# A planner's costs raised a little for each ScalarE, VectorE and GpSimd instruction and each DMA

## The chip, the cores and the metric

The kernel runs on one core of one Trainium2 chip. The metric is the device time of one execution in microseconds (us), the median of several runs. Engines are named as in the profile: PE (TensorE matmuls), PEld (its weight loads), ACT (ScalarE), DVE (VectorE), POOL (GpSimd), SP (SyncE, which issues the DMAs).

## The reference

```python
q_n, k_n = rmsnorm(q, g_q), rmsnorm(k, g_k)            # q, k, v: 4 batches, 12 heads, 448 x 64
attn = softmax(q_n @ k_n.T / sqrt(64))                 # the row maximum is subtracted first
x = (attn @ v).transpose(0, 2, 1, 3).reshape(1792, 768)
h = maximum(x @ w_in, 0); x = (h * h) @ w_out          # first MLP, 768 -> 2048 -> 768
h = x @ w_in2                                          # second MLP, same sizes
out = (maximum(h, 0) + alpha * minimum(h, 0)) @ w_out2
```

## The kernel before

All data is 32-bit. A product of two fp32 matrices is made of three fp32r matmuls: each operand is split into a high part (a copy that rounds) and a low part (the rest), and high x high, high x low and low x high are added in PSUM. So nearly every matrix needs a copy (L254 on ACT, L258 on DVE, L256 on POOL) and a subtraction (L262 on DVE or POOL) before PE may read it. A matmul has 128x128 weights and 448 columns, one batch's tokens.

The program has two parts. `with_attention` does attention for the four batches, head by head: norms (L528 to L611), spreading of the norm factors (L636, L641), splitting of q and k into tiles `mv` and `st` (L254, L262), a matmul for the row maximum (L685) that DVE reduces (L689), transposes (L692), scores (L710), exponentials (L718), the product with v (L729 in fp32, L753 in three parts) and the division (L766 to L783). Between these stand the matmuls of the first MLP for batches 0 and 1 (L350, `bank<-xs,whl` and `bank<-hg,whl`). They are PE's other work while a head waits for ACT and DVE. Their weights come in units. The first time, a unit is loaded (`raw`), converted by ACT (L282) and four DVE instructions (L286, L289, L293, L296) into `ws`, split by L254 and L262 into `whl`, and written back to DRAM. Later uses load the split form. The first pass has 56 units, on average 10.3 matmuls each (32 of 9 and 24 of 12).

`without` does the first MLP for batches 2 and 3 (L350, `m<-...`), and then the second MLP in two stages, first for batches 0 and 1, then for 2 and 3. A stage forms 2x2 blocks and takes seven products instead of eight: steps "up" (u0 to u7) and "down" (d0 to d2, each of three quads) of seven products of six or nine matmuls (L984), into PSUM banks `n`. Between the products ACT copies banks out (L254, `q<-n`, `ws<-n`), DVE adds (L995) and applies alpha (L1022), and the sums are split into `forms`. Weight sums are L908. `x_pair` prepares a stage's input: it loads four blocks of the first MLP's result `y` (`q<-y`, `ws<-y`), and with DVE or POOL subtractions (L995) and splits (L254, L262) makes seven forms in `xs` and `xt`. It does so three times for a stage. Copies of banks and loads of `y` take their space from one pool, `q`, of nine slots; those whose space lies in the old `ws` tile are printed as `ws`. The second stage's inputs are prepared while PE does the last step of the first, d2: I call this place the join.

No order is written by hand. `Tasks.add` records every instruction with an urgency, the engines that can do it and the time it is expected to take (`act`, `dve`, `dve2`, `pool1`, `pool2`, `load`, `MM` = 0.202). `Tasks.run` (L104 to L187) plays them through on a model with one clock for each engine: among the tasks that can begin soonest it takes the most urgent, gives it an engine and buffer slots, and sets when the engine is free (`ends`) and when the result may be used (`t.end` plus WAIT). Instructions are emitted in that order. On the chip each engine then works its list from the top; the times of the model have no other part in it.

```python
WAIT = {"T": 0.27, "A": 0.17, "V": 0.17, "P": 0.17, "S": 0.1}
s = max(s, d.end + (0 if d.engine == e == "T" else self.WAIT[e]))
t.end = self.ends[e] = s + t.on[e]
```

Of the kernel before, what the change touches and what calls it, by code (L numbers as in the profile page):

```python
# [52 lines left out]
class Tasks:  # L53
    WAIT = {"T": 0.27, "A": 0.17, "V": 0.17, "P": 0.17, "S": 0.1}

    PRICE = {"A": 1.5, "V": 3.5, "P": 1.5}
# [44 lines left out]
    def run(self, phase=0):  # L101
# [16 lines left out]
        while left:  # L118
# [42 lines left out]
            if e == "S" and t.on[e]:  # L161
                self.ends[e] = s + 0.06
                self.dma = max(self.dma, s + 1.3) + t.on[e]
                t.end = self.dma + 0.8
            else:
                t.end = self.ends[e] = s + t.on[e]
                self.gap[e] = t.gap
                if e in t.alone:
                    self.port = t.end
# [49 lines left out]
def attention_relu2_mlp_prelu_mlp(ctx: ExitStack, tc: tile.TileContext, qkt, qk_tm, v, gb, alpha, ident, sel,  # L219
# [199 lines left out]
    def with_attention():  # L419
        with ExitStack() as es:  # L420
# [70 lines left out]
            def attention(b, base, first=False):  # L491
# [17 lines left out]
                def first_norms(pairs, urgency, r):  # L509
# [3 lines left out]
                    for p in pairs:  # L513
                        src, sq = load_qk(p), Buf(pool=here("pf"))
                        for i in range(2):
# [3 lines left out]
                            def square(e, src=src, rows=rows, i=i):  # L519
# [6 lines left out]
                            n = steps.index((p, i))  # L526
                            add(urgency, {"T": 4 * MM},
                                lambda e, n=n, rows=rows: nc.tensor.matmul(  # L528
# [25 lines left out]
                def norms(gr):  # L554
# [57 lines left out]

                    add(urgency, {"T": 0.4}, transposes, [t1, ident_b], [pr])
                    for o in (0, 64):
# [64 lines left out]
                def shift(h):  # L679

                    m, s, mc, mn = mvs[h], sts[h], Buf(pool="mc"), Buf(pool="mn")
                    for t in range(NCH):
# [8 lines left out]
                    pt = Buf(pool="bank")  # L691
                    add(at(h, -19), {"T": 0.1}, lambda e: nc.tensor.transpose(pt.ap[:NCH, :CP], mc.ap, ident_b.ap),  # L692
                        [(mc, t) for t in range(NCH)], [pt])
# [5 lines left out]
                def head(h):  # L699
                    p, j = divmod(h, 2)  # L700
                    m, s, o = mvs[h], sts[h], Buf(pool="pv")
                    for n in range(NCH):
# [17 lines left out]
                        if p not in vparts:  # L720
                            if n % 2 == 0:
                                pf = Buf(pool=here("pf"))

                            def pfv(pf=pf, c=n % 2 * S, keys=keys):
                                return pf.ap[:keys, c:c + S]

                            add(g, {"A": act(S, True)}, exp(pfv), [pa], [(pf, n % 2)], "exp")
                            add(at(h, 5 + n), {"T": 4 * MM},
                                lambda e, n=n, pfv=pfv, keys=keys: nc.tensor.matmul(  # L729
                                    out=o.ap[:, :S], lhsT=vs[p].ap.bitcast(F32)[:keys, 192 * n + 64 * j:192 * n + 64 * j + 128], rhs=pfv(),  # L730
                                    start=(n == 0), stop=(n == NCH - 1)), [(pf, n % 2), vs[p]], [o], "pv")
                            continue
# [515 lines left out]
```

## Time and profile before

| | us |
|---|---|
| median of 3 runs (1257.81 to 1262.97) | 1258.88 |
| the profiled execution | 1263.64 |
| its span | 1261.9 |
| PE busy | 1193.9 (95%) |
| DVE busy | 890.5 (71%) |
| ACT busy | 771.2 (61%) |
| POOL busy | 506.9 (40%) |

Busy PE isn't PE at its peak, since matmuls are pipelined and a waiting one can look busy; the number of matmuls in a stretch is the better measure. PE has 5466 records, of which 1008 are of the group L984 `n<-forms,whl`. The chain that ended last is 60% PE, 20% DVE, 9% ACT, 7% DMA.

### The profile page before, as it was taken

Reading aid. Unit: us, or ns where it says so; the run is one execution under the profiler, and the core shown is the slowest. Engines: PE = TensorE matmul, PEld = TensorE weight load, DVE = VectorE, ACT = ScalarE, POOL = GpSimd, SP = SyncE. Lnnn points to the kernel's source line nnn. Section 1 sums busy time; section 2 is a strip of 40 time slices with the busy share of each in tenths; the row PEclk is TensorE's granted clock in tenths of the full one; section 3 lists DMA queues with packets and bytes.
Section 4 is the critical chain, followed back from the end, with each engine's and each line's share of the span. In section 5 each row is a group of like instructions: output and inputs, shape, how many; then the busy total and the mean of one; then the engine's idle time right before and its main releaser. Section 6 shows DMA issues by size and latency. Waiting matters only on the chain.

```text
span 1261.9 us, 17161 instructions
## 1 busy us (share of the span) xinstructions
PE 1193.9 (95%) x5466; PEld 1006.7 (80%) x5466; DVE 890.5 (71%) x1593; ACT 771.2 (61%) x1543; POOL 506.9 (40%) x469
## 2 busy tenths in 40 slices
PE   4898999999999999999999999999999979999998
PEld 2555676666679888898989999888989869898987
DVE  6888999989996864603787661088776996847483
ACT  5787789777778777822555311376746745654472
POOL 4345345564355323310000002864676743317255
PEclk7998999999999999999999999999999989999999
DMA  6325767677754445267999996482616548261632
GB/s 203 101 82 179 235 240 276 217 267 257 243 213 133 158 150 174 91 204 255 320 342 308 320 362 207 169 277 96 251 50 241 184 141 260 77 200 52 211 109 81
DMA packets 95803, 250.32 MB, mean 198 GB/s; under 512 B 11296, under 2 KB 30880, under 8 KB 95712
## 3 DMA queue, kind: packets, MB, share of 16 engines
q1 hardware_dynamic: 95712, 249.22, 58.1%
q8 instruction: 43, 0.70, 0.2%
q14 instruction: 48, 0.39, 0.1%
HBM read 178.32 MB, written 70.78 MB: 197 GB/s over the span
## 4 chain that ended last, share of the span: by engine, by line
PE 60%; DVE 20%; ACT 9%; DMA 7%; issue 3%; SPq 0%; POOL 0%; ACTq 0%; DVEq 0%
PE n L984 23%; PE m L350 14%; PE bank L350 10%; PE pv L729 4%; PE bank L710 4%; DMA raw<-in_w 3%; DVE mc L689 2%; PE pv L753 2%; DVE n L995 2%; PE bank L685 2%; DMA whl<-w 2%; DVE ws L293 2%; DVE ws L296 2%; DVE ws L286 1%; ACT forms L254 1%
## 5 line engine op out<-in xcount | busy, mean ns | idle before, releaser
L984 PE MATMUL n<-forms,whl 128*128 128x448 f32 x1008 | 212.4, 371 | 17.1 <-ACT ws L254 7.2
L984 PEld LDWEIGHTS n<-forms,whl 128*128 128x128 f32 x1008 | 190.7, 190 | 37.7 <-DVE forms L262 8.1
L350 PE MATMUL bank<-xs,whl 128*128 128x448 f32 x576 | 137.9, 379 | 0.4 <-DMA whl<-w 0.4
L350 PE MATMUL bank<-hg,whl 128*128 128x448 f32 x576 | 130.1, 367 | 0.8 <-DMA whl<-w 0.8
L984 PE MATMUL n<-xs,whl 128*128 128x448 f32 x576 | 123.1, 367 | 1.5 <-ACT ws L254 1.2
L262 POOL TENSOR_TENSOR whl<-ws,whl 128x384 fp32r<-128x384 f32 (+2 forms) x56 | 79.9, 1430 | 105.7 <-ACT whl L254 99.0
L350 PEld LDWEIGHTS bank<-xs,whl 128*128 128x128 f32 x576 | 108.5, 191 | 16.2 <-issue 4.2
L282 ACT ACTIVATE ws<-raw 128x384 f32<-128x384 f32 (+1 forms) x112 | 67.2, 600 | 85.7 <-DMA raw<-in_w 75.1
L350 PE MATMUL m<-xs,whl 128*128 128x448 f32 x576 | 118.3, 367 | 1.0 <-ACT q L254 0.7
L350 PE MATMUL m<-hg,whl 128*128 128x448 f32 x576 | 119.2, 368 | 0.0
L689 DVE TENSOR_REDUCE mc<-bank 112x1 f32<-112x448 f32 x192 | 109.8, 615 | 10.7 <-PE bank L685 9.5
L984 PEld LDWEIGHTS n<-xs,whl 128*128 128x128 f32 x576 | 107.8, 188 | 11.8 <-issue 1.5
L350 PEld LDWEIGHTS m<-xs,whl 128*128 128x128 f32 x576 | 107.9, 188 | 11.3 <-ACT q L254 1.1
L350 PEld LDWEIGHTS m<-hg,whl 128*128 128x128 f32 x576 | 108.1, 188 | 10.9
L350 PEld LDWEIGHTS bank<-hg,whl 128*128 128x128 f32 x576 | 107.3, 188 | 11.1 <-DMA whl<-w 1.5
L262 POOL TENSOR_TENSOR whl<-raw,whl 128x384 fp32r<-128x384 f32 (+1 forms) x87 | 90.0, 1038 | 51.1 <-ACT whl L254 43.1
L286 DVE TENSOR_SCALAR ws<-ws 128x384 f32<-128x384 f32 (+1 forms) x112 | 48.8, 442 | 86.2 <-ACT ws L282 85.8
L710 PE MATMUL bank<-mv,st 128*112 128x448 f32 (+2 forms) x352 | 102.1, 398 | 6.0 <-DVE mc L689 3.8
L262 POOL TENSOR_TENSOR xs<-q,xs 128x448 fp32r<-128x448 f32 x11 | 13.2, 1211 | 234.9 <-ACT xs L254 234.9
L254 ACT ACTIVATE whl<-raw 128x384 fp32r<-128x384 f32 (+1 forms) x123 | 60.7, 500 | 57.1 <-PE n L984 44.4
L984 PE MATMUL n<-xt,whl 128*128 128x448 f32 x432 | 94.0, 367 | 1.7 <-DVE q L995 1.2
L984 PEld LDWEIGHTS n<-xt,whl 128*128 128x128 f32 x432 | 80.8, 188 | 9.8 <-DVE q L995 1.6
(173 smaller groups left out, 2301.0 us busy)
## 6 DMA issues: line engine op xcount, KB each, us to landing
raw<-in_w SPq DMA_DIRECT2D x64, 384.0 KB
raw<-in_w SPq DMA_DIRECT2D x48, 512.0 KB
whl<-w SPq DMA_DIRECT2D x64, 384.0 KB
whl<-w SPq DMA_DIRECT2D x48, 512.0 KB
k_u<-whl SPq DMA_DIRECT2D x56, 384.0 KB
whl<-k_u SPq DMA_DIRECT2D x56, 384.0 KB
w<-whl SPq DMA_DIRECT2D x32, 384.0 KB
w<-whl SPq DMA_DIRECT2D x24, 512.0 KB
```

What stands on the lines that cost most here:

```text
L254: nc.scalar.activation(out=o, in_=i, func=ACTF.Copy)
L262: (nc.gpsimd if e == "P" else nc.vector).tensor_tensor(out=o, in0=x, in1=hi, op=ALU.subtract)
L282: lambda e: nc.scalar.activation(out=f.ap[:, :n], in_=half(1).bitcast(F32), func=ACTF.Abs), [raw], [f], "f")
L286: lambda e: nc.vector.tensor_scalar(out=f.ap[:, :n], in0=f.ap[:, :n], scalar1=TINY, scalar2=None, op0=ALU.max),
L293: lambda e: nc.vector.scalar_tensor_tensor(out=fu(), in0=half(1), scalar=0xC0000000, in1=fu(), op0=ALU.bitwise_and, op1=ALU.bitwise_or), [ ...
L296: lambda e: nc.vector.scalar_tensor_tensor(out=fu(), in0=half(0), scalar=29, in1=fu(), op0=ALU.logical_shift_right, op1=ALU.bitwise_or), [ ...
L350: nc.tensor.matmul(out=acc.ap[:, t, :S], lhsT=w.ap[:, part * n + 128 * kk:part * n + 128 * kk + 128], rhs=src(h, k0 + kk, t)[1](), start=( ...
L685: lambda e, t=t, pm=pm: nc.tensor.matmul(out=pm.ap[:CP, :S], lhsT=m.ap[:, 0, t * CP:(t + 1) * CP], rhs=s.ap[:, 0, :], start=True, stop=Tru ...
L689: lambda e, t=t, pm=pm: nc.vector.reduce_max(out=mc.ap[:, t:t + 1], in_=pm.ap[:CP, :S], axis=AX.X),
L710: nc.tensor.matmul(out=pa.ap[:keys, :S], lhsT=s.ap[:rows, k, c:c + keys], rhs=m.ap[:rows, k, :], start=(k == 0), stop=(k == 1))
L729: lambda e, n=n, pfv=pfv, keys=keys: nc.tensor.matmul(out=o.ap[:, :S], lhsT=vs[p].ap.bitcast(F32)[:keys, 192 * n + 64 * j:192 * n + 64 * j ...
L984: nc.tensor.matmul(out=psum(x), lhsT=w.ap[:, part * n + 128 * kk:part * n + 128 * kk + 128], rhs=get(h)[1](), start=fresh and h == 1, stop ...
```

## The change

A table LATE is added (in us), and its number goes onto the end of every task that takes time. On ACT, DVE and POOL the engine is also held longer (`ends`). For a DMA only the result comes later. Four PE tasks get other numbers: an fp32 matmul 0.751 instead of 0.808, two transposing tasks 0.32 instead of 0.4 and 0.035 instead of 0.1. No instruction's work changes; what changes is the order, which engine takes a task that several can do, and which slot a buffer gets. All line numbers from L56 on rise by 2.

```diff
     WAIT = {"T": 0.27, "A": 0.17, "V": 0.17, "P": 0.17, "S": 0.1}
+
+    LATE = {"T": 0.0, "A": 0.04, "V": 0.04, "P": 0.1, "S": 0.25}
...
-                t.end = self.dma + 0.8
+                t.end = self.dma + 0.8 + self.LATE[e]
             else:
-                t.end = self.ends[e] = s + t.on[e]
+                t.end = self.ends[e] = s + t.on[e] + self.LATE[e] * (t.on[e] > 0)
...
-                            add(urgency, {"T": 4 * MM},
+                            add(urgency, {"T": 0.751},
...
-                    add(urgency, {"T": 0.4}, transposes, [t1, ident_b], [pr])
+                    add(urgency, {"T": 0.32}, transposes, [t1, ident_b], [pr])
...
-                    add(at(h, -19), {"T": 0.1}, lambda e: nc.tensor.transpose(pt.ap[:NCH, :CP], mc.ap, ident_b.ap),
+                    add(at(h, -19), {"T": 0.035}, lambda e: nc.tensor.transpose(pt.ap[:NCH, :CP], mc.ap, ident_b.ap),
...
-                            add(at(h, 5 + n), {"T": 4 * MM},
+                            add(at(h, 5 + n), {"T": 0.751},
```

The first place is ACT at the join. `q_4644<-n_6534` copies the first product of d2's second quad out of its bank, and `ws<-n_6539` the second product; `xs` and `xt` rows are splits of prepared input. Before:

```order
L254 ACTIVATE q_4644<-n_6534 128x448
L254 ACTIVATE whl<-wf_6529 128x384 x2
L254 ACTIVATE xs_62<-q_6532 128x448
L254 ACTIVATE whl<-raw 128x384
L254 ACTIVATE xs_62<-ws 128x448
L254 ACTIVATE xs_63<-ws 128x448
L254 ACTIVATE xt_4639<-ws 128x448
L254 ACTIVATE ws<-n_6539 128x448
```

After, on ACT at the same place (the first product is copied to `q_6533`, the third by the last row):

```order
L256 ACTIVATE q_6533<-n_6540 128x448
L256 ACTIVATE xs_63<-q_4642 128x448
L256 ACTIVATE xt_4641<-q_4643 128x448
L256 ACTIVATE xt_4640<-q_4645 128x448
L256 ACTIVATE ws<-n_6539 128x448
L256 ACTIVATE whl<-wf_6529 128x384
L256 ACTIVATE xs_62<-q_4644 128x448
L256 ACTIVATE q_4642<-n_6540 128x448
```

Ahead of the second copy stand three splits of the first `x_pair` instead of seven instructions, four of which are splits of the second `x_pair`, whose `y` blocks are loaded late.

The second place is DVE at the join: from `sums_out<-n_...`, the last addition of d2's first quad, to the first addition of its second quad (`...<-n_6539`). Before there are 20 instructions between the two, among them four L908; these rows are the last eleven and the addition:

```order
L995 TENSOR_TENSOR ws<-ws,q_6532 128x448
L262 TENSOR_TENSOR xs_62<-q_6532,xs_62 128x448
L262 TENSOR_TENSOR xs_62<-ws,xs_62 128x448
L262 TENSOR_TENSOR xs_63<-ws,xs_63 128x448
L262 TENSOR_TENSOR xt_4639<-ws,xt_4639 128x448
L995 TENSOR_TENSOR ws<-ws 128x448
L995 TENSOR_TENSOR q_6532<-ws,q_6532 128x448
L995 TENSOR_TENSOR ws<-ws 128x448
L262 TENSOR_TENSOR xs_63<-ws,xs_63 128x448
L262 TENSOR_TENSOR xt_4641<-q_6532,xt_4641 128x448
L262 TENSOR_TENSOR xt_4640<-ws,xt_4640 128x448
L995 TENSOR_TENSOR ws<-n_6539,ws 128x448
```

After, on DVE, from the one addition to the other (12 instructions between):

```order
L997 TENSOR_TENSOR sums_out<-n_6534,sums_out 128x448
L264 TENSOR_TENSOR xt_4639<-ws,xt_4639 128x448
L997 TENSOR_TENSOR q_4642<-q_4642,ws 128x448
L260 CAST whl<-wf_6529 128x384
L997 TENSOR_TENSOR q_4643<-q_4642,q_4643 128x448
L997 TENSOR_TENSOR q_4645<-q_4645,q_4642 128x448
L264 TENSOR_TENSOR xs_63<-q_4642,xs_63 128x448
L264 TENSOR_TENSOR xt_4641<-q_4643,xt_4641 128x448
L264 TENSOR_TENSOR xt_4640<-q_4645,xt_4640 128x448
L910 TENSOR_TENSOR raw<-raw 128x384 x3
L997 TENSOR_TENSOR ws<-ws,q_4644 128x448
L997 TENSOR_TENSOR q_4642<-n_6539,q_4642 128x448
```

The work of the second `x_pair` has moved behind the addition, and a copy of weights (CAST) has come to DVE.

The third place is PE where batch 1's first heads begin; L685 (after: L687) is a head's matmul for the maximum, L350 (L352) the first MLP's. Before:

```order
L350 MATMUL bank_158<-xs_62,whl 128x448 x12
L685 MATMUL bank_159<-st_167,mv_163 112x448
L685 MATMUL bank_156<-st_167,mv_163 112x448
L350 MATMUL bank_158<-xs_62,whl 128x448 x3
L685 MATMUL bank_159<-st_167,mv_163 112x448
L350 MATMUL bank_157<-xs_62,whl 128x448 x3
L685 MATMUL bank_156<-st_167,mv_163 112x448
L350 MATMUL bank_157<-xs_62,whl 128x448 x3
```

After, on PE at the same place:

```order
L352 MATMUL bank_157<-xs_62,whl 128x448 x12
L687 MATMUL bank_156<-st_167,mv_163 112x448
L687 MATMUL bank_159<-st_167,mv_163 112x448
L687 MATMUL bank_156<-st_167,mv_163 112x448
L352 MATMUL bank_157<-xs_62,whl 128x448 x3
L687 MATMUL bank_159<-st_167,mv_163 112x448
L352 MATMUL bank_160<-xs_62,whl 128x448 x6
L687 MATMUL bank_156<-st_168,mv_164 112x448
```

Three of the first head's matmuls now stand together, and six MLP matmuls instead of three stand between the last of them and the second head's first. Counted in the order, the first MLP runs further ahead of attention later on: between the last L685 of the 24th head and that of the 32nd there are 252 MLP matmuls instead of 156.

## Rows read from the trace of the kernel before

**Rows 1.** Page, busy time of PE, share of the span, instructions

```profile
PE 1193.9 (95%) x5466; PEld 1006.7 (80%) x5466; DVE 890.5 (71%) x1593; ACT 771.2 (61%) x1543; POOL 506.9 (40%) x469
```

**Rows 2.** Stretches: length, busy PE, PEld, DVE, ACT, POOL, TensorE clock, DMA share, GB/s

```profile
115.00:355.00 240.00, 222.73 (x920) 163.48 (x921) 222.57 (x424) 190.81 (x396) 117.53 (x101) 0.98 0.70 242
355.00:580.00 225.00, 221.49 (x1077) 194.17 (x1075) 128.21 (x221) 150.56 (x313) 72.19 (x72) 1.00 0.50 162
580.00:818.00 238.00, 237.01 (x1153) 216.05 (x1152) 129.68 (x248) 91.69 (x136) 33.81 (x30) 1.00 0.85 291
...
990.00:1030.00 40.00, 29.93 (x130) 26.45 (x129) 35.58 (x53) 22.74 (x46) 21.98 (x19) 0.87 0.32 112
```

**Rows 3.** Timeline of PE at the join: start, length, work [idle before, releaser]

```profile
998.35 17.39 PE L984 MATMUL n<-forms,whl 128*128 128x448 f32 x75 [2.80 <-DVE forms L262]
1022.91 7.37 PE L984 MATMUL n<-forms,whl 128*128 128x448 f32 x27 [7.16 <-ACT ws L254]
```

**Rows 4.** Timeline of ACT at the join

```profile
1012.19 0.54 ACT L254 ACTIVATE q<-n 128x448 f32<-128x448 f32 x1 [1.50 <-PE n L984]
...
1016.54 1.14 ACT L254 ACTIVATE xs<-ws 128x448 fp32r<-128x448 f32 x2 [0.39 <-DMA ws<-y]
...
1022.31 0.54 ACT L254 ACTIVATE ws<-n 128x448 f32<-128x448 f32 x1 [2.16 <-DVE ws L995]
```

**Rows 5.** Timeline of DVE at the join

```profile
1010.30 0.62 DVE L995 TENSOR_TENSOR sums_out<-n,sums_out 128x448 f32<-128x448 f32 x1 [0.15 <-PE n L984]
...
1014.22 3.38 DVE L908 TENSOR_TENSOR raw<-raw 128x384 f32<-128x384 f32 x3
...
1021.61 0.61 DVE L995 TENSOR_TENSOR ws<-ws 128x448 f32<-128x448 f32 x1
```

**Rows 6.** Timeline of SP's queue behind the join

```profile
1028.79 0.34 SPq L265 DMA_DIRECT2D out_t<-sums_out  x1
1029.22 0.38 SPq L265 DMA_DIRECT2D q<-y  x1
```

**Rows 7.** Timeline of POOL at the join

```profile
1027.37 1.39 POOL L995 TENSOR_TENSOR sums_out<-sums_out,ws 128x448 f32<-128x448 f32 x1 [10.65 <-DVE ws L995]
```

**Rows 8.** Stretches of 10 us at the join, columns as in rows 2

```profile
1020.00:1030.00 10.00, 7.09 (x27) 6.43 (x28) 8.35 (x15) 4.62 (x10) 1.54 (x2) 0.68 0.04 13
1030.00:1040.00 10.00, 10.00 (x50) 9.09 (x49) 10.00 (x15) 6.08 (x13) 5.77 (x4) 1.00 0.64 202
```

**Rows 9.** Timeline of DVE: two copies of weights and a weight sum

```profile
834.62 0.35 DVE L258 CAST whl<-raw 128x384 fp32r<-128x384 f32 x1
...
992.89 1.17 DVE L258 CAST whl<-raw 128x384 fp32r<-128x384 f32 x1
...
996.45 0.55 DVE L908 TENSOR_TENSOR raw<-wf 128x384 f32<-128x384 f32 x1
```

**Rows 10.** Timeline of PE, first stage of the second MLP

```profile
832.09 2.09 PE L984 MATMUL n<-xt,whl 128*128 128x448 f32 x9 [1.19 <-DVE q L995]
...
918.15 4.09 PE L984 MATMUL n<-forms,whl 128*128 128x448 f32 x18 [1.15 <-DVE forms L262]
```

**Rows 11.** Timeline of DVE in the first 20 us

```profile
17.67 1.27 DVE L587 TENSOR_REDUCE ss<-tm 112x8 f32<-112x512 f32 x2
18.86 0.67 DVE L550 SCALAR_TENSOR_TENSOR rhl<-rhl,columns,r 128x448 fp32r<-128x448 f32 x1
```

**Rows 12.** PE's longest wait from 115 to 355: total us, times, longest

```profile
PE bank L685 <- ACT mv L254: 4.5, 1, 4.5
```

**Rows 13.** Groups of DVE's weight conversion: busy us, mean ns | idle before

```profile
L296 DVE SCALAR_TENSOR_TENSOR ws<-raw,ws 128x384 uint32<-128x384 uint32 (+1 forms) x112 | 71.3, 643 | 2.0
L293 DVE SCALAR_TENSOR_TENSOR ws<-raw,ws 128x384 uint32<-128x384 uint32 (+1 forms) x112 | 69.6, 628 | 1.9
L286 DVE TENSOR_SCALAR ws<-ws 128x384 f32<-128x384 f32 (+1 forms) x112 | 48.8, 442 | 86.2 <-ACT ws L282 85.8
L289 DVE TENSOR_SCALAR ws<-ws 128x384 uint32<-128x384 uint32 (+1 forms) x112 | 47.7, 432 | 2.1
```

## The prediction

> **What bounds the kernel now.** I read the page's busy times first: PE is busy for 1193.9 of 1261.9 us [rows 1], so 68.0 us are visible waits, and no other engine is near it. The matmuls stay the same, so only PE's waits and the clock that it is granted can change. Then I read the stretches, to see where the waits lie. From 580 to 818, where PE runs from one list of matmuls, 1153 of them take 238 us, 0.206 us each; the sparsest stretch is 990 to 1030, with 130 in 40 us, PE busy for 29.93 us, and a mean clock of 0.87 [rows 2]. From 115 to 355 PE is idle for 240 - 222.73 = 17.3 us, and DVE is busy for 222.57 of 240 us [rows 2]: there attention and the first MLP's weight conversion fill DVE. From 355 to 580 DVE is busy for 128.21 of 225 us, and PE is idle for only 3.5 us.
>
> Third, the timelines of the worst stretch, the join. PE waits twice, 2.80 us for a DVE split and 7.16 us for an ACT copy out of a bank [rows 3]. The second wait can be followed. The copy `ws<-n` at 1022.31 stands behind splits `xs<-ws` that had to wait for a DMA of `y` until 1016.54, and itself waited for a DVE subtraction `ws<-ws` [rows 4], because that frees its space in the pool `q`. The subtraction came at 1021.61, behind three weight sums that took 3.38 us from 1014.22 [rows 5]. So PE waits for space, and the space is late because preparation of the next stage stands ahead of it. POOL meanwhile waited 10.65 us [rows 7].
>
> **The change part by part.** The planner's numbers cost nothing on the chip; the order does. Shown as rows in the section on the change: the join on ACT and DVE, and the first heads of batch 1 on PE.
>
> *The join.* On ACT the second quad's second copy no longer has the second `x_pair` ahead of it, only three splits of the first, whose `y` blocks are there long before. On DVE 12 instead of 20 instructions stand between two additions that PE needs. What goes: the 7.16 us wait. With it the slow clock: in 1020 to 1030 the mean granted clock is 0.68, with 27 matmuls in that stretch [rows 8], the first at 1022.91 [rows 3]. At 0.206 us they would take 5.6 of the 7.1 us to 1030, so 1.5 us are the half-speed level's (1.2 instead of 2.4 GHz). PE had waited for 7.16 us before. The first wait, 2.80 us, ends with a DVE split, and ahead of that split one CAST and one L908 have moved away: 1.17 and 0.55 us [rows 9], 1.7 us. Together 7.16 + 1.5 + 1.7 = 10.4 us.
>
> What is late next is DVE: it was busy for 35.58 of 40 us at the join [rows 2], which leaves 4.4 us, and for 10.00 of 10 us just behind [rows 8]. The last `y` loads were issued at 1029.22, right behind an output store at 1028.79 [rows 6] that waited for the additions which POOL began at 1027.37 [rows 7]; this chain moves forward with PE. Of the 8.7 us by which PE would be early behind the long wait, 4.4 fit into DVE's idle time; of the other 4.3 I give half back, 2.1 us, since sums for the output can slide and splits can't. The join's term is -8.3 us. Its ends: -10.4 if nothing is late, and +3.5 if the wait stays and the three more CASTs that DVE gets there each cost the longer 1.17 us.
>
> *Smaller places of the second MLP.* Before u0's first addition of the first stage DVE has one more split and one more L908, about 0.55 us each [rows 9], and PE waited for that addition already (1.19 us [rows 10]): +1.1. In u4 of that stage one split and one CAST more stand in the chain that ended PE's wait of 1.15 us [rows 10]: 0.55 + 0.35 = +0.9. In u4 of the second stage one L908 more, +0.55; in u2 of the first one split and a CAST fewer and one L908 more, -0.35. At the start one of two 0.64 us reductions that stood ahead of L550 moves behind it [rows 11]: -0.6. Sum +1.6; if PE's other work hides the additions, -1.0, and if casts cost 1.17 each, +2.4.
>
> *Attention.* The order of some thousand matmul rows changes, and no row prices that. The bounds: -17.3 us if every wait from 115 to 355 goes [rows 2], and from above the conversion. Between the 24th and the 32nd head 96 more MLP matmuls run; at 10.3 a unit that is 9.3 units more, with 0.643 + 0.628 + 0.442 + 0.432 = 2.15 us of DVE each [rows 13], 20 us on a full engine. I take -3 us. The longest wait, 4.5 us for the first heads of batch 1 [rows 12], keeps its twelve MLP matmuls of cover and hardly changes. Further on wider cover stands between the heads, and some attention moves from the full stretch to the one where DVE has 97 us to spare [rows 2], which speaks for a small gain, nearer to the wait of 4.5 us than to either end.
>
> *The sum.* -8.3 + 1.6 - 3 = -9.7 us, which on the profiled execution's 1263.6 us gives 1253.9. That execution was 4.8 us above the median of the runs, so I predict 1258.9 - 9.7 = **1249.2 us**. Ends of all terms together would be 1230 and 1285; not all fall on one side.
>
> *A rule weighed.* Seven copies of weights or inputs move to DVE in all (31 CASTs become 38). One of them alone took 0.35 us; another, at the join, 1.17 us [rows 9]. The Trainium skill (SBUF — State Buffer, section "Who interferes with whom") says that DVE and GpSimd share one pair of ports, that a cast can take it for its whole length, and that the later of the two then waits fully. The two lengths agree with it, but no row here sets a pair of such instructions side by side. By the rule the sum would be higher, as the fourth rival says.
>
> **The rivals.**
>
> 1. *The wait moves.* DVE is the join's engine, 10.00 of 10 us busy behind it [rows 8], so PE gets through the second quad early and waits for `xs` and `xt` at the next stage's start. For it: 20 instructions have become 12 in one place only because eight stand later. Against: DVE's order now serves PE first, and output sums can slide. Then the join gives nothing: 1258.9 + 1.6 - 3 = 1257.5.
> 2. *DVE is overloaded in attention.* The first MLP runs ahead, its conversion is packed into the stretch where DVE is 93% busy [rows 2], and PE stands at L350 for `whl`. Price 20 us instead of -3: 1258.9 - 8.3 + 1.6 + 20 = 1272. It decides from about 13 us on, where it outweighs the join by over 0.5%. For it: the four instructions take 2.15 us [rows 13]. Against: PE has 96 x 0.206 = 19.8 us more work in the same stretch, so DVE's share hardly rises, and now L685 waits, not L350 [rows 12].
> 3. *The plan fits attention better than I grant.* Half of the 17.3 us goes instead of 3: 1258.9 - 8.3 + 1.6 - 8.6 = 1243.6. For it: only the order makes PE wait there. Against: DVE is full.
> 4. *The copies on DVE collide.* Seven casts at 1.17 - 0.35 = 0.82 us more [rows 9], all on the path: +5.7, 1254.9. Against: ACT is relieved of as many, and most casts run ahead of need.
> 5. *The change does nothing.* The rows of the order rule that out as a cause; as a time it is in the first.
>
> **How the numbers follow.** My forecast has 0.47 (its own range is 1242 to 1256), the moved wait 0.17, the overload 0.17, the better fit 0.14, the collision 0.05. A measurement of this kernel can tell some 0.5% from no change: faster is below 1252.6, slower above 1265.2. Of my own case 0.41 lies below 1252.6 and 0.06 in between. Faster: 0.41 + 0.14 = 0.55. Same: 0.06 + 0.17 + 0.05 = 0.28. Slower: 0.17. The range reaches down past the better fit to 1238 and up to 1266, which leaves out most of the overload and the tail of the better fit, 2 in 10.
>
> **What would show it.** In the changed profile: between the last step of the first stage and the second stage PE has no wait of over 3 us, the clock stays at its full level there, and that step's 130 matmuls take about 31 us instead of 40 [rows 2]. PE's visible waits fall from 68 to about 58 us. The `y` loads of the third `x_pair` are issued sooner behind the first ones. From 115 to 355 PE's idle time is between 10 and 18 us. I am wrong if a wait of 5 us or more stands at the second stage's u0, if L350 (then L352) waits for `whl` from DVE or POOL, or if the first MLP's end on PE comes with more idle time than before.

## The result

The changed kernel takes 1266.13 us (median of 20 runs, 1260.96 to 1270.61), the kernel before 1258.18 us beside it (20 runs, 1255.21 to 1269.16): a ratio of 1.0055, 95% interval 1.0039 to 1.0072. It is slower by 7 us (8 us between the two medians), where 1249.2 us had been forecast, and the time lies just above the range. A second set of 12 runs gave 1266.02 us, 1.0054 (1.0033 to 1.0075).

The profiled execution of the changed kernel took 1260.96 us, and that of the kernel before 1263.64 us: by these two alone the change would be a gain. The one is the fastest of its 20 runs, the other 5.5 us above its median. The two traces can show where PE waits, but not which kernel is faster.

### The profile after

In the changed kernel every line from 56 on has a number that is 2 higher. First the row of PE from the page (busy us, share, instructions), which answers to [rows 1]:

```profile
PE 1184.8 (94%) x5466; PEld 1014.5 (81%) x5466; DVE 890.8 (71%) x1597; ACT 771.9 (61%) x1542; POOL 506.5 (40%) x466
```

PE's visible waits are 1259.2 - 1184.8 = 74.4 us, where they were 68.0. The windows of [rows 2] and [rows 8], with the same columns:

```profile
115.00:355.00 240.00, 225.70 (x958) 174.30 (x959) 219.83 (x419) 186.71 (x385) 110.46 (x88) 0.98 0.74 251
355.00:580.00 225.00, 222.82 (x1095) 198.69 (x1094) 131.70 (x232) 157.38 (x329) 77.83 (x80) 1.00 0.53 164
990.00:1030.00 40.00, 33.41 (x140) 27.95 (x139) 37.37 (x51) 19.59 (x40) 27.18 (x21) 0.91 0.39 125
...
1020.00:1030.00 10.00, 8.36 (x40) 6.99 (x38) 8.32 (x8) 4.40 (x9) 9.33 (x7) 1.00 0.57 185
1030.00:1040.00 10.00, 6.52 (x31) 5.67 (x31) 8.93 (x18) 4.29 (x8) 3.27 (x2) 1.00 0.51 165
```

In attention PE is idle for 14.3 us instead of 17.3. From 1020 to 1030 the clock is full and 40 matmuls run instead of 27, as forecast; but in the 10 us behind that only 31 run instead of 50, and from 990 to 1030 the mean granted clock is 0.91, so the slow level has not left the join. The timeline of PE through the join (start, duration, operation, the wait before it and what ended it) answers to [rows 3]:

```profile
991.50 2.70 PE L986 MATMUL n<-forms,whl 128*128 128x448 f32 x12 [1.12 <-DVE forms L264]
995.36 0.68 PE L986 MATMUL n<-forms,whl 128*128 128x448 f32 x2 [1.16 <-ACT whl L256]
996.48 6.89 PE L986 MATMUL n<-forms,whl 128*128 128x448 f32 x25 [0.44 <-POOL whl L264]
1003.85 7.78 PE L986 MATMUL n<-forms,whl 128*128 128x448 f32 x36 [0.47 <-DVE ws L997]
1013.38 13.33 PE L986 MATMUL n<-forms,whl 128*128 128x448 f32 x56 [1.75 <-ACT ws L256]
1028.36 1.71 PE L986 MATMUL n<-forms,whl 128*128 128x448 f32 x7 [1.65 <-POOL whl L264]
1032.18 2.10 PE L986 MATMUL n<-forms,whl 128*128 128x448 f32 x9 [2.12 <-ACT q L256]
1035.64 4.54 PE L986 MATMUL n<-forms,whl 128*128 128x448 f32 x21 [1.36 <-ACT ws L256]
```

The wait of 7.16 us is gone. Eight shorter ones stand there, and they add up to 10.07 us; the two of [rows 3] were 2.80 + 7.16 = 9.96 us. The time did not leave the join, it was dealt out again.

What is new stands 140 us earlier, in d0 of the first stage. PE in the changed kernel:

```profile
846.14 4.08 PE L986 MATMUL n<-forms,whl 128*128 128x448 f32 x18
854.70 1.86 PE L986 MATMUL n<-forms,whl 128*128 128x448 f32 x4 [4.49 <-ACT whl L256]
```

and in the kernel before, at the same matmuls:

```profile
860.55 4.20 PE L984 MATMUL n<-forms,whl 128*128 128x448 f32 x18
866.14 10.21 PE L984 MATMUL n<-forms,whl 128*128 128x448 f32 x49 [1.39 <-ACT sums_out L254]
```

What PE waits for is the split weights of d0's fourth product. The chain on DVE and then on ACT in the changed kernel:

```profile
852.14 1.68 DVE L264 TENSOR_TENSOR forms<-n,forms 128x448 fp32r<-128x448 f32 x3
853.73 0.41 DVE L910 TENSOR_TENSOR raw<-wf,raw 128x256 f32<-128x256 f32 x1
```

```profile
852.60 0.55 ACT L256 ACTIVATE forms<-n 128x448 fp32r<-128x448 f32 x1
854.23 0.42 ACT L256 ACTIVATE whl<-raw 128x256 fp32r<-128x256 f32 x1 [1.08 <-issue]
```

The fourth weight sum, `raw<-wf,raw`, stands behind the splits of u2; ACT copies its result 0.1 us after it and PE starts behind the copy. In the kernel before the same sum ran ahead of those splits, 8.6 us before PE began that product:

```profile
857.13 0.42 DVE L908 TENSOR_TENSOR raw<-wf,raw 128x256 f32<-128x256 f32 x1
```

And PE's wait for DVE's splits 15 matmuls into d1, 1.15 us in [rows 10], is longer:

```profile
910.63 14.59 PE L986 MATMUL n<-forms,whl 128*128 128x448 f32 x62 [2.56 <-DVE forms L264]
```

The matmuls of the second MLP stand in the same sequence in all kernels of this study, so a stretch can be measured from the start of its first matmul to that of the next stretch's first (the last one to the start of the last matmul). This takes in waits and clock, and does not depend on where a window falls. Worked out from the timelines of PE, in us, with two profiles of each of the two kernels:

```
stretch (matmuls)  u0-u2  d0    u3-u4  d1    u5-u7  d2=join  stage 2  second
                   189    126   126    189   189    189      1008     MLP
before             41.1   27.6  25.6   39.9  38.6   52.6     211.6    437.1
before, again      41.1   27.6  25.6   39.9  38.7   53.8     211.7    438.4
after              42.7   33.2  25.5   43.3  39.0   54.1     213.9    451.7
after, again       42.7   33.2  25.5   42.7  38.7   53.7     215.7    452.2
```

Two profiles of one kernel agree here within 1.8 us, and the change costs 14 us: 5.6 at d0, 3 at d1, 1.6 at u0 to u2, about 1 at the join, 2 to 4 in the second stage.

These are not waits alone. The windows of d0, d1 and the join, first in the kernel before and then in the changed kernel, with the columns of [rows 2]:

```profile
860.55:888.15 27.60, 26.09 (x127) 23.51 (x126) 21.81 (x46) 16.74 (x38) 12.19 (x15) 1.00 0.26 93
913.80:953.70 39.90, 38.75 (x190) 35.34 (x189) 30.15 (x46) 18.12 (x37) 30.44 (x25) 1.00 0.24 89
992.35:1044.99 52.64, 42.58 (x190) 37.89 (x189) 48.21 (x71) 28.16 (x57) 28.91 (x23) 0.90 0.41 133
```

```profile
846.14:879.34 33.20, 28.71 (x127) 25.70 (x126) 24.69 (x51) 16.06 (x36) 11.87 (x13) 0.90 0.22 76
904.88:948.21 43.33, 40.77 (x190) 36.69 (x189) 27.93 (x46) 18.86 (x39) 27.95 (x24) 0.96 0.23 82
987.18:1041.23 54.05, 43.98 (x190) 37.37 (x189) 49.85 (x72) 26.70 (x54) 33.38 (x26) 0.94 0.43 138
```

At d0 PE's waits grow by 3.1 us (4.49 for 1.39), and the same matmuls keep it busy for 2.6 us longer, at a mean granted clock of 0.90 instead of 1.00. At d1 the waits grow by 1.4 us and the busy time by 2.0, at 0.96 instead of 1.00. So a stretch at the lower clock level comes with the longer waits; by PE's busy time it costs about as much again (an estimate, since a waiting PE can look busy).

The time up to the second MLP's first matmul is not so steady: 819.5 and 813.7 us before, 803.4 and 808.7 after. For the first part only medians of many runs serve.

### The profile page after: what moved, and what is told of

Read it like the earlier page. It is cut to its first block, busy times and chain, and to the rows that moved or that the text cites. A ratio compares the mean times of both kernels' runs of the same rounds, so it can differ in the third digit from the quotient of the medians.

```text
span 1259.2 us, 17184 instructions
## 1 busy us (share of the span) xinstructions
PE 1184.8 (94%) x5466; PEld 1014.5 (81%) x5466; DVE 890.8 (71%) x1597; ACT 771.9 (61%) x1542; POOL 506.5 (40%) x466
## 4 chain that ended last, share of the span: by engine, by line
PE 72%; DVE 16%; ACT 6%; DMA 3%; issue 3%; POOL 0%; SPq 0%; ACTq 0%; DVEq 0%; POOLq 0%
PE n L986 24%; PE m L352 19%; PE bank L352 13%; PE bank L712 5%; PE pv L731 5%; PE pv L755 3%; PE bank L687 2%; DVE mc L691 2%; DVE n L997 1%; DVE raw L910 1%; ACT forms L256 1%; DVE ws L295 1%; DVE forms L264 1%; DVE mv L264 1%; DVE ws L298 1%
## 5 line engine op out<-in xcount | busy, mean ns | idle before, releaser
L986 PE MATMUL n<-forms,whl 128*128 128x448 f32 x1008 | 218.3, 377 | 22.7 <-DVE forms L264 7.1
L986 PEld LDWEIGHTS n<-forms,whl 128*128 128x128 f32 x1008 | 193.9, 194 | 46.1 <-DVE forms L264 8.6
L352 PE MATMUL bank<-xs,whl 128*128 128x448 f32 x576 | 141.0, 377 | 1.1 <-DVE mv L264 1.1
L352 PE MATMUL bank<-hg,whl 128*128 128x448 f32 x576 | 131.0, 369 | 0.3 <-DMA whl<-w 0.3
L352 PEld LDWEIGHTS bank<-xs,whl 128*128 128x128 f32 x576 | 109.6, 193 | 15.1 <-issue 2.5
L264 POOL TENSOR_TENSOR whl<-raw,whl 128x384 fp32r<-128x384 f32 (+1 forms) x90 | 93.0, 1039 | 63.3 <-ACT whl L256 50.1
L352 PE MATMUL m<-xs,whl 128*128 128x448 f32 x576 | 117.0, 365 | 0.7 <-ACT q L256 0.7
L352 PEld LDWEIGHTS bank<-hg,whl 128*128 128x128 f32 x576 | 107.5, 188 | 12.4 <-issue 2.6
L352 PE MATMUL m<-hg,whl 128*128 128x448 f32 x576 | 116.9, 365 | 0.0
L352 PEld LDWEIGHTS m<-xs,whl 128*128 128x128 f32 x576 | 108.1, 188 | 9.6 <-ACT q L256 1.1
L352 PEld LDWEIGHTS m<-hg,whl 128*128 128x128 f32 x576 | 108.2, 188 | 8.5
L288 DVE TENSOR_SCALAR ws<-ws 128x384 f32<-128x384 f32 (+1 forms) x112 | 46.2, 417 | 79.0 <-ACT ws L284 78.6
L997 POOL TENSOR_TENSOR q<-q,q 128x448 f32<-128x448 f32 x7 | 8.4, 1205 | 225.8 <-DMA q<-y 225.6
L256 ACT ACTIVATE whl<-raw 128x384 fp32r<-128x384 f32 (+1 forms) x115 | 57.1, 500 | 68.0 <-PE n L986 47.2
```

Source lines behind the costliest of these rows:

```text
L256: nc.scalar.activation(out=o, in_=i, func=ACTF.Copy)
L264: (nc.gpsimd if e == "P" else nc.vector).tensor_tensor(out=o, in0=x, in1=hi, op=ALU.subtract)
L288: lambda e: nc.vector.tensor_scalar(out=f.ap[:, :n], in0=f.ap[:, :n], scalar1=TINY, scalar2=None, op0=ALU.max),
L352: nc.tensor.matmul(out=acc.ap[:, t, :S], lhsT=w.ap[:, part * n + 128 * kk:part * n + 128 * kk + 128], rhs=src(h, k0 + kk, t)[1](), start=( ...
L986: nc.tensor.matmul(out=psum(x), lhsT=w.ap[:, part * n + 128 * kk:part * n + 128 * kk + 128], rhs=get(h)[1](), start=fresh and h == 1, stop ...
L997: return lambda e: (nc.gpsimd if e == "P" else nc.vector).tensor_tensor(out=out(), in0=i0(), in1=i1(), op=op)
```

## The experiments

Theories at the start: W, the loss is in the second MLP, where weight work now stands behind splits; D, DVE is overloaded in attention; E, it is one execution's chance. Each kernel was timed against the kernel before on the same chip. Two costs can be set apart, since the plan of the first part (attention and first MLP) is made before that of the second.

### One part of the change alone

`att_only` sets the added time to zero behind the first part's plan:

```
             ts.run()
+            ts.LATE = {"T": 0.0, "A": 0.0, "V": 0.0, "P": 0.0, "S": 0.0}
```

> The raised costs are used only while the first part (attention with the first MLP of batches 0 and 1) is planned; behind it the table is set to zero, so PE's order there is that of the changed kernel and the later part is planned with the old costs. Theory W (the loss lies in the second MLP, where weight work was put behind the splits of forms and PE then waits for the weights): faster than before, 1245 to 1253 us. Rival D (DVE overloaded in attention): slower, 1262 to 1270. Rival E (the two traces differ only by the execution that was profiled): 1258 to 1263, PE's waits before 580 us as in before.

Measured: 1254.0 us, 0.9965 (0.9949 to 0.9982), faster. Second MLP 436.9 us.

`mlp2_only` is the converse: old costs in the first part, the added time set behind it.

> The reverse: the old costs while the first part is planned (PE's order there is exactly that of before), the raised costs from the first MLP of batches 2 and 3 on. Theory W: slower than before by 8 to 14 us, 1266 to 1272, with waits for whl at the beginning of a down step. Rival D: 1252 to 1259. Rival E: 1258 to 1263.

Measured: 1267.2 us, 1.0068 (1.0041 to 1.0095), slower; second MLP 448.3 us, with 33.1 at d0. So D falls and W has its place: the first part gains about 4.4 us, the second loses 8.6 us (or, from 1.0055/0.9965, 11 us; the stretches of the profiles above say 14 us, and the three are not reconciled). The changed kernel was timed once more beside these:

> The changed kernel once more, for a second profiled execution beside the times. Theory W: 1264 to 1268, and the waits in the second MLP stand at the same places as in the first profile (the fourth product of d0 for ACT whl, over 3 us). Rival E: the long waits stand elsewhere.

It gave 1.0054, and in its profile the wait at d0's fourth product is there again, 4.48 us. The kernel before was profiled once more too (one run, 1259.11 us): its two waits at the join stand there again, 2.82 and 7.19 us. E falls.

### Is it the wait at d0?

`d0_sums` lowers one urgency in the changed kernel, so that the four sums of d0 come ahead of u2's splits; in DVE's order some two dozen rows move, all around that place.

```
-                    add(urgency, {"V": dve(n)},
+                    add(urgency - 30 * (urgency == 40004), {"V": dve(n)},
```

> The changed kernel with one number more: the four weight sums of the first down quad of the first stage (d0, 128x256 sums at L910) get an urgency that is 30 lower, so that the fourth sum, raw<-wf,raw, stands on DVE ahead of the block of additions and splits of u2 instead of behind it. The rest of the order is as in the changed kernel but for about a dozen rows around that place. Theory W (what the second MLP loses lies in waits of PE for weights that the plan put behind splits): the wait of 4.5 us for ACT whl at the fourth product of d0 goes, and the time falls by 4 to 4.6 us, to about 1261.8, ratio to the kernel before 1.002. Rival M (the wait only moves: the splits of u2, now later by what the sums take, make PE wait ahead of the first product on forms): the time stays at 1266, ratio 1.0055, with a new wait of 3 us or more within 15 us of the place.

Measured: 1262.46 us, 1.0033 (1.0006 to 1.0059). In its trace the wait of 4.49 us is gone; behind the same 18 matmuls PE waits 0.56 us and 24 matmuls later 2.00 us:

```profile
857.89 5.13 PE L986 MATMUL n<-forms,whl 128*128 128x448 f32 x24 [0.56 <-ACT sums_out L256]
865.02 7.16 PE L986 MATMUL n<-forms,whl 128*128 128x448 f32 x34 [2.00 <-DVE sums_out L997]
```

The d0 stretch takes 28.6 us instead of 33.2, at a granted clock of 1.00 again. That is W's local part. The time agrees with W's 1261.8, but the interval holds 1.0055 too, and the second MLP in that profile (452.6 us; 55.8 at the join, 219.2 in stage 2) did not get shorter. Shown is the cause of the wait; that the whole 4.5 us reach the end is not.

### Half and twice the added time in the second part

> The first part is planned as in the changed kernel, the second part (second MLP) with half the added time per instruction and DMA. In this order the fourth sum of d0 stands ahead of the splits of u2 again. Base is the kernel with nothing added in the second part, ratio 0.9965. Theory W: no wait of 4.5 us at d0; the other places of the second MLP fall as its order happens to, and the time is 1254 to 1262. Rival G (the loss grows with the time that the plan adds): half of the second part's loss of 0.9 per cent is there, spread over many small waits: 1259.5, ratio 1.001. A time above 1264 speaks against both.

> As the run before, with twice the added time in the second part. The fourth sum of d0 stands behind the splits of u2, as in the changed kernel. Theory W: the wait of 4.5 us at d0 is there, other places as the order happens to fall: 1260 to 1270, and not steadily worse than with the single amount. Rival G: twice the second part's loss, 0.9965 + 2 x 0.009 = 1.0145, 1277.

Measured: half 1262.2 us, 1.0018 (0.9994 to 1.0041); twice 1270.87 us, 1.0086 (1.0053 to 1.0119). Over a first part of 0.9965 the second part loses 0 (by definition), 0.53, 0.90 and 1.21% for none, half, all and twice. So it is more than one unlucky place: G's direction holds, though the growth is less than in proportion, and W's "not steadily worse" does not. The intervals of half and all touch, and so do those of all and twice; none against any of them, and half against twice, are clear of noise. The wait at d0 is there where the order said it would be. With half the added time the sum stands ahead of the splits, and PE has no wait for `whl` there; with twice, behind them:

```profile
851.93 1.88 PE L987 MATMUL n<-forms,whl 128*128 128x448 f32 x6 [1.51 <-ACT whl L256]
856.48 15.88 PE L987 MATMUL n<-forms,whl 128*128 128x448 f32 x69 [2.66 <-ACT whl L256]
```

With half it is the join (58.3 us) and d1 (43.8) that lose. With half and with twice a long wait stands at the join again (7.28 and 6.90 us): that it is gone in the changed kernel belongs to this one amount.

### All weight work earlier

`weights_first` moves the urgency of every weight sum and copy of the second MLP ahead of the splits of two quads before:

```
-                made = None if key in kept7 else sums(n, group, t0 - 24)
+                made = None if key in kept7 else sums(n, group, t0 - 48)
...
-                        w = unit(name, n, made, t0 + j - 17, None, None)
+                        w = unit(name, n, made, t0 + j - 41, None, None)
```

> The changed kernel in which the urgencies of all weight sums and weight copies of the second MLP are 24 lower (three quads sooner), so that they rank ahead of the splits and additions of the two quads before. Theory W, in its general form (the added time makes more tasks compete in the plan, urgency then decides, and weight work that ranks behind splits comes late): the loss of the second part goes, no wait for whl of over 1.5 us is left behind 800 us, and the time is 1252 to 1259, ratio below 1.000. Rival X (DVE is short of time as a whole there, and weights taken first make the splits late instead): 1264 or above, with PE's waits on forms, xs and xt longer.

Measured: 1267.71 us, 1.0069 (1.0045 to 1.0092). d0 falls to 29.7 us, but u5 to u7 take 40.5 and the join 56.1. W as a general rule falls. Its forecast of no long wait for `whl` fails as well, for one stands at the join:

```profile
1024.04 2.54 PE L986 MATMUL n<-forms,whl 128*128 128x448 f32 x7 [4.41 <-DVE whl L264]
```

X's time fits, but 1.0069 can't be told from the changed kernel's 1.0055. In this profile, most of what the weights win at d0 is lost at u5 to u7 and at the join.

### What the join's time consists of

All runs on the join but the last start from a plan without added time in the second part: `join_later` and `join_pool` from `att_only` (1254.0 us), the others from `late1_only` (1252.69 us; it stands further down). The join takes 52.4 us in both. `join_later` and `join_sooner` change when the loads of `y` for the second stage may start:

```
-for k, n in enumerate((-57, -39, -24)):
+for k, n in enumerate((-54, -36, -21)):     # later
+for k, n in enumerate((-60, -42, -27)):     # sooner
```

> The kernel with nothing added in the second part (1254.0, ratio 0.9965), in which the long wait of 7.3 us at the join still stands; here the loads of y for the second and third x_pair, and so what ACT and DVE do with them, may start 3 products later each (begun -54, -36, -21 instead of -57, -39, -24). Theory J (the long wait is one of space in q that the x_pair work holds, and goes when that work comes later): the 7.3 us wait goes, and no more than 3 us come back behind it: 1247 to 1250, ratio 0.992. Rival K (the join's work on DVE is what takes the time, so a long wait that goes comes back as several shorter ones, as in the changed kernel): the waits from 975 to 1050 stay at 14 us or more in sum, 1252 to 1257.

Measured: 1259.31 us, 1.0006 (0.9984 to 1.0028), 0.4% slower than its base; the join takes 58.4 us, with the long wait still there.

> Base as before (1252.7), full work; the loads of y for the second stage may start three products sooner each (begun -60, -42, -27), the mirror of the run that let them start three later, which was 0.4 per cent slower than its base. Theory N: the work then competes with more of the first stage and with less of the second; the 7.3 us wait shrinks by 2 us or more and the time falls to 1249 to 1251. Rival B (the amount of work in that stretch is what counts, and any shift of the loads only re-deals it): within 3 us of 1252.7 on either side.

Measured: 1260.12 us, 1.0006 (0.9990 to 1.0023), 58.8 us at the join. The long waits of the later and of the sooner loads:

```profile
1020.49 15.32 PE L987 MATMUL n<-forms,whl 128*128 128x448 f32 x63 [7.93 <-ACT ws L256]
1038.62 7.30 PE L987 MATMUL n<-forms,whl 128*128 128x448 f32 x27 [2.81 <-ACT q L256]
```

```profile
1008.62 12.89 PE L987 MATMUL n<-forms,whl 128*128 128x448 f32 x54 [6.90 <-ACT ws L256]
1031.13 8.03 PE L987 MATMUL n<-forms,whl 128*128 128x448 f32 x27 [4.86 <-ACT q L256]
```

Both shifts keep a wait of 7 to 8 us, and the waits at the join grow from 10 or 11 us to 13.5 and 15.1 us. J and N's forecast for the loads fall, and so does B's, that a shift costs nothing.

`join_pool` gives the splits of the second `x_pair` group to GpSimd alone:

```
-add(urgency, {"V": dve(S), "P": pool2(S)}, lambda e: rest(...
+add(urgency, {"P": pool2(S), **({"V": dve(S)} if batches == (0, 1) else {})}, lambda e: rest(...
```

> The kernel with nothing added in the second part (ratio 0.9965, 1254), in which the splits of the second x_pair group (batches 2 and 3) may go to GpSimd alone; DVE has 21 rows fewer in all, GpSimd 24 more, most of them at the join. Theory K (DVE is what takes the time at the join, whatever the order): PE's waits from 975 to 1050, 14.8 us in the base, fall by 5 us or more, 1246 to 1250. Rival Q (the space in q and the loads of y set the join, not DVE): GpSimd's 1.1 us for each instead of 0.55 us holds the space longer, the waits stay or grow, 1254 to 1262.

Measured: 1265.41 us, 1.0047 (1.0030 to 1.0064); join 61.9 us, and u0 to u2 of stage 2 take 42.3 instead of 38.3:

```profile
1014.69 3.52 PE L987 MATMUL n<-forms,whl 128*128 128x448 f32 x9 [8.17 <-ACT q L256]
1036.78 7.29 PE L987 MATMUL n<-forms,whl 128*128 128x448 f32 x27 [2.83 <-ACT ws L256]
1051.07 0.87 PE L987 MATMUL n<-xs,whl 128*128 128x448 f32 x3 [2.14 <-POOL xs L264]
```

K falls: DVE with 21 instructions fewer did not help, and GpSimd holds the space longer, as Q has it; the loss is larger than Q's. `more_q` has four buffers in `q` where two were added, and one fewer in `whl`:

```
-more("whl", 2, [128, 2 * S], F32R)     more("q", 2, [128, S], F32)
+more("whl", 1, [128, 2 * S], F32R)     more("q", 4, [128, S], F32)
```

> Base as before, full work; in the second phase two more buffers in the pool q (a 128x448 value each) and one fewer in whl (a pair of split weights), which is the same space. Theory Q (the long wait is one of space in q, as the subtraction that freed it for the copy out of the bank showed): the wait of 7.3 us at the join goes or falls below 3 us, 1245 to 1249, unless the fewer whl make PE wait for weights elsewhere. Rival Y (the wait is for engine time, not space): the wait stays at 6 us or more, 1252 to 1257.

Measured: 1264.64 us, 1.0042 (1.0024 to 1.0060). The long wait is gone, as Q has it, and the join takes 47.1 us, 5.3 less than its base. But stage 2 then begins with

```profile
1042.23 1.49 PE L987 MATMUL n<-xs,whl 128*128 128x448 f32 x3 [5.85 <-POOL xs L264]
```

and its first stretch takes 47.3 us instead of 38.3; d1 and u5 to u7, with a `whl` fewer, lose 5.5 us. The long wait is one of space in `q`. Whether more space would also save time is not shown, since this run pays for it with a `whl`.

`no_pair` leaves the `x_pair` work of the second stage out altogether, and `no_pair_late` does the same with the added time in the second part.

> Base is the best version so far: old TensorE numbers, added time in the first part alone (1252.7, ratio 0.9958). Left out: the whole x_pair work of the second stage (12 loads of y, 33 splits and copies, 12 subtractions); the second stage reads the forms of the first, so its outputs are those of the other batches. Theory N (what costs at the join is that this work and the seventh-weight and up-quad work stand on the same engines and in the same space at once): the waits of 7.3 and 3.0 us go, PE's waits from 975 to 1050 fall from 14.7 to under 6 us, 1242 to 1245, ratio 0.988. Rival Y (the join waits for the weights or additions of the last two quads themselves): over 10 us of waits stay there, 1249 or above.

Measured: 1244.23 us, 0.9884 (0.9865 to 0.9903). The join takes 42.4 us instead of 52.4. The window from 985 to 1035 in the base (`late1_only`) and then here, with the columns of [rows 2], and the one long wait that is left there:

```profile
985.00:1035.00 50.00, 41.37 (x185) 37.25 (x186) 45.59 (x67) 23.95 (x49) 27.42 (x20) 0.90 0.45 149
```

```profile
985.00:1035.00 50.00, 47.00 (x228) 42.27 (x227) 31.71 (x48) 19.95 (x40) 29.16 (x25) 1.00 0.42 143
```

```profile
992.52 8.17 PE L987 MATMUL n<-forms,whl 128*128 128x448 f32 x39 [2.82 <-DVE forms L264]
```

PE runs 43 matmuls more in those 50 us, and DVE is busy for 31.71 instead of 45.59 us. N's numbers hold. Over the whole join PE's waits fall from 9.8 to 3.0 us, and the mean granted clock rises from 0.90 to 1.00. Whether it is the engines, the space or the loads that this work takes from d2, the run can't tell, since all of it goes at once.

> As the run before, with the added time in the second part as the changed kernel has it; the same work is left out. It asks how much of what the added time costs in the second part (0.7 to 0.9 per cent, 9 to 11 us) lies in the order at the join. If all of that is at d0, u4 and other places away from the join (4.5 + 2.5 + 4 us), the difference to the run before stays 8 us or more. If the join's competition is a main part of it, the difference falls to 5 to 6 us, what is left being the wait of 4.5 us at d0 and that at u4.

Measured: 1252.16 us, 0.9945 (0.9928 to 0.9961): 7.9 us above the run before, with the same 42.5 us at the join. In the two profiles the second MLP takes 437.8 and 426.7 us. So the added time costs 8 us (11 in the profiles) where there is nothing to win or lose at the join: 33.1 instead of 27.5 at d0, 42.7 instead of 39.9 at d1, 42.6 instead of 41.1 at u0 to u2.

### Which number helps the first part

`t_only` keeps the four TensorE numbers and adds no time anywhere; `late1_only` adds the time in the first part and keeps the old TensorE numbers.

> Of the change only the four TensorE numbers (0.751 for the products that read float32, 0.32 and 0.035 for transposes); nothing is added to the other engines' instructions or to DMAs anywhere. The second MLP's plan has the old costs. Theory T (the first part gains since PE's plan is truer): about the ratio of the run with the first part alone, 0.9965, 1254. Rival L (it gains since the loads and copies are counted later): 1.000 or above, 1258 to 1263.

> Of the change only the added time, and that in the first part alone; the four TensorE numbers are the old ones, the second part has the old costs. Theory T: 1.000 or above. Rival L: 0.9965 or below, 1254. If both this run and the one with the TensorE numbers alone lie near 1.000, neither number does it by itself.

Measured: 1265.8 us, 1.0046 (1.0026 to 1.0067), and 1252.69 us, 0.9958 (0.9936 to 0.9979). T falls, L holds, though `t_only` came out slower than L had it. The TensorE numbers alone make the first part slower; the added time makes it faster, with or without them. `late1_only` is faster than both kernels of this case, as is `att_only`; between these two nothing is settled. Nor were the entries of the table (ACT and DVE, POOL, DMA) tried one by one.

## Why the prediction was wrong

*The join, -8.3 us.* This step failed. Its mechanism was read rightly: the 7.16 us wait was one for space in `q`, and the new order took it away. The error was to count the wait, with the slow clock behind it, as time that the new order saves. In the changed kernel 10.07 us of shorter waits stand there, the mean granted clock is 0.94 where I had it full (0.90 before), and the stretch takes 54 us instead of 53. `no_pair` measures what the stretch costs: 10 us, the `x_pair` work of the second stage beside d2. Five kernels dealt that work out anew: three kept a wait of 7 to 8 us and added others, the changed kernel cut it in pieces, and `more_q` pushed it into stage 2. I had let 4.4 us fit into DVE's idle time and given back half of the rest; but over the join DVE is idle for 4.2 us in the changed kernel and was for 4.4 before, so that hardly any of it was room. This is the first rival's result by another way: the wait moved, though not to the next stage's start: in the changed kernel no wait stands at the second stage's u0.

*Smaller places of the second MLP, +1.6 us.* This step failed too, and weighs more: 8 us by the runs without the pair, 11 us in their profiles. Of the places I priced, the first up quad and u4 moved as I said, but more (u0 to u2 +1.6 us for +1.1 - 0.35; d1 +3 us for the +0.9 of u4). The largest was none of mine: the sum of d0's weights, a wait of 4.49 us, with which d0 takes 5.6 us more. In the order, that sum was a row that had gone from ahead of a block of splits to behind it. Ahead of the splits at the join I counted such a row as 0.55 us won, and never asked when the row itself was needed. I also gave these places no price for the clock, which I had done at the join: it fell to 0.90 at d0 and to 0.96 at d1.

*Attention, -3 us.* Right in size, but partly by luck, since no row priced it: the first part gives -0.35% (-0.51 to -0.18), 4.4 us, and PE's idle time from 115 to 355 is 14.3 us, within the 10 to 18 named. The longest wait there, which I said would hardly change, became 5.79 us; in the faster `late1_only` it is 7.99 us. A longest wait is no measure of its stretch. The overload that the second rival feared did not come: DVE is busy for 219.83 us from 115 to 355. By which waits the added time helps there is not shown.

*The sum.* The base, the median of the runs, was right: it came out at 1258.18 us. With -4.4 and +8.6 to +11 for its terms the same sum gives 1262 to 1265, near the time measured.

*The chances.* The only rival that ended slower put it in attention. None had the second MLP lose more than the +1.6 us, although DVE was 10.00 of 10 us busy just behind the join [rows 8] and the change moves rows there as much as anywhere. The fourth rival's price did not come either: all casts on DVE together take 18.0 us instead of 15.8.

What stays open: why the added time hurts the second MLP at every amount. That weight work loses rank when more tasks are ready at once in the plan fits d0, but `weights_first` shows that rank alone does not mend it. Nor is it much more work for DVE: from the second MLP's first matmul on it is busy for 319.3 us before and 321.4 after (319.5 and 323.8 in the second profiles). What makes the waits at u0 to u2 and d1 longer was not tried by a run of its own, and `d0_sums` leaves open how much of d0's loss reaches the end.

## What to carry to other kernels

A wait that goes is a gain only if the engines and buffers behind it have room for the work that it held up: take the suspected work out altogether once, and see what the stretch costs without it. A planner's cost can be right for one stretch alone: the same added time gave 4 us in one part of this program and took 9 in the other, so try it part by part. In a change of order, ask of each row that moves back who needs its result and when, before counting what it no longer delays, and price a wait together with the slower clock behind it; and compare fixed pieces of work in two traces, not two single executions.

## What the runs showed of the hardware

DVE's additions and splits of 128x448 that read two SBUF tensors take up to two and a half times as long while GpSimd runs an addition or split of its own. DVE and then POOL in the changed kernel, at the join:

```profile
1021.76 1.58 DVE L264 TENSOR_TENSOR xs<-q,xs 128x448 fp32r<-128x448 f32 x1
1023.27 0.61 DVE L997 TENSOR_TENSOR sums_out<-n,sums_out 128x448 f32<-128x448 f32 x1
...
1028.71 1.57 DVE L264 TENSOR_TENSOR xt<-q,xt 128x448 fp32r<-128x448 f32 x1
1030.20 0.61 DVE L264 TENSOR_TENSOR xs<-ws,xs 128x448 fp32r<-128x448 f32 x1
```

```profile
1021.46 1.40 POOL L997 TENSOR_TENSOR sums_out<-sums_out,q 128x448 f32<-128x448 f32 x1 [0.46 <-DVE q L997]
1022.83 1.54 POOL L264 TENSOR_TENSOR xs<-ws,xs 128x448 fp32r<-128x448 f32 x1
...
1028.27 1.53 POOL L997 TENSOR_TENSOR q<-q,ws 128x448 f32<-128x448 f32 x1
```

Beside POOL the split takes 1.58 us, alone 0.61; the addition at 1023.27, which reads `n` in PSUM, takes 0.61 us beside POOL's split. In the second MLP of the changed kernel 27 such instructions with two SBUF inputs overlap one of POOL by 0.2 us or more, median 1.42 us, and 16 don't, 0.62 us; of those with one input in PSUM 124 overlap, median 0.62 us. In the kernel before 21 with two SBUF inputs overlap, median 0.96 us. The Trainium skill (SBUF — State Buffer, section "Who interferes with whom") says that a DVE instruction with two SBUF inputs contends with GpSimd's reads and one with at most one SBUF input, outside the two-port modes, does not; these rows agree. My prediction had priced only casts that way. For them too the changed kernel has rows: its 19 casts on DVE that overlap no instruction of POOL take 0.28 to 0.36 us, and all 11 of over 0.4 us, up to 1.32, overlap one.
